# Attention beside a token-mixing MLP on one core: where a unit's dense matmuls stand

## The chip, the cores and the metric

The kernel runs on one core of a Trainium2 chip. The metric is the device time of one execution in microseconds. Three runs of the kernel before gave 650.64, 650.80 and 651.08; the median, 650.8, is the time before.

The core has five engines with a queue of instructions each: TensorE (PE in the profile, PEld for its weight loads), VectorE (DVE), ScalarE (ACT), GpSimd (POOL) and SyncE (SP), which here issues nearly all DMAs. The engines tell each other with semaphores when something is done.

## The reference

The input x has 2048 tokens of 1024 columns. Its layernorm `xn` goes through two blocks, and the sum is returned. Cut to what matters:

```python
xn = _layernorm(x)
# A: 32 heads of 32 columns, 4 segments of 512 tokens
q, k, v = xn @ wq, xn @ wk, xn @ wv
for s in range(4):
    p = softmax(q_s @ k_s.T * scale + causal_mask)
    a_dot = p @ v_s
    a_mem = (phi(q_s) @ M) / (phi(q_s) @ z + 1e-6)     # phi(t) = t + 1 if t > 0 else exp(t)
    o_s = g * a_mem + (1 - g) * a_dot                  # g = sigmoid(beta), per head
    M, z = M + phi(k_s).T @ v_s, z + sum(phi(k_s))
A = concat(o_s) @ wo
# B: an MLP across tokens, 2048 -> 3584 -> 2048, for each column
B = (gelu(layernorm(xn).T @ w1 + b1) @ w2 + b2).T
return x + A + B
```

## The kernel before, in words

The program has two large parts in time. Until about 387 us it computes the MLP (and the keys of the last two segments). From there on it runs attention, and only attention is touched by the change.

**Units.** Attention goes through 32 units (`N_UNIT`), u = 8 s + g: segment s of four, group g of four heads out of eight. In `attention` (the loop over `u`) each unit has:

- its logits, `logits(u, step)`: keys times queries into banks 0 to 3 of PSUM. Step 0 and step 1 belong to the unit, step 2 is done once for an even unit and its successor together. After the matmuls ScalarE takes the exp of all four banks into `pT` (line 1370, 128x2048), GpSimd masks the diagonal blocks (line 1374), and `late_exps` (line 1219, tile `etmp`) takes the exp that phi needs for every Q or K product that has ended since the last logits.
- the weighing of the unit before, `weigh(u - 1, 0..2)`: `pT` times the values, and phi(q) times the memory, into banks 4 and 5, which VectorE evacuates (lines 1424 and 1427, tile `ost`).
- the normalising of the unit before, `combine(u - 1)`, on VectorE: reciprocals, a product (line 1473, `prod`), an add (line 1479, `o_s`). Then a DMA transposes `o_s` into `oT`.
- dense jobs, eight matmuls of 128x512 each, which fill TensorE while ScalarE works on the exps.

**Dense jobs.** `unit_jobs(u)` says which jobs a unit adds to the queue `self.jobs`: a V product of the next segment (`v_job`), the Q product of unit u + 2 (`q_job`), its K product in the first two segments (`k_job`; later keys are loaded by `k_load`), and products of finished segments with wo (`wo_job`). From unit 18 (`QUOTA_FROM`) wo products are appended until the unit has 24 matmuls if even and 20 if odd; what the last of them has over the quota (`self.left`) is carried into the next unit. The last unit takes all that remains.

Jobs run in the order of the queue, in pieces: `dense(n)` takes the next n matmuls, whatever jobs they belong to. The loop calls it between the other pieces of the unit, and the sizes n come from `cut(total, shares)`, which divides the unit's matmuls by fixed shares. The seven shares of an even unit are for the places before logits 0, before `weigh` 0, 1 and 2, before logits 1, before logits 2, and after it; an odd unit has no logits 2 and six shares.

**Banks and evacuations.** A dense job takes bank 6 or 7 in turn when its first matmul is issued. When its eighth matmul is issued the job's `end` is emitted: the evacuation of its bank. V and (from the third segment on) all Q products are evacuated by ScalarE (lines 1299 and 1253), wo products by VectorE, which adds the product to a tile `fin` (line 1313) that already holds the residual and the MLP. A job's first matmul waits, by the bank's bookkeeping in `FW._waits`, for the evacuation of the job two before it. The end of a Q product also asks for the next weights of `wq` (`ring.ensure(u + 2)`), and puts the exp for phi on the list of `late_exps`.

**Side work.** Pieces of VectorE work of the unit (`combine`, phi of the queries in `phi_q`, scaling of later tokens) wait in `self.side`. After logits 1, `dense` pops one of them each time a job has reached one of its stops (`STOPS_FEW` in these units: after matmuls 1, 3, 5 and 7 of a job that ScalarE evacuates, after 1, 3 and 5 of one that VectorE evacuates). So the order of the jobs also sets the order of instructions on VectorE, ScalarE and the DMA queue. All queues are written out in this order when the program is built.

After unit 31 `tail` does the weighing of that unit and the wo products of the last segment.

Of the kernel before, what the change touches and what calls it, by code (L numbers as in the profile page):

```python
# [30 lines left out]
N_UNIT = N_SEG * N_GRP  # L31
# [355 lines left out]
class _Kernel:  # L387
# [1119 lines left out]
    def unit_jobs(self, u):  # L1507
        jobs = [self.wo_job(*self.wo_jobs.popleft())] if 10 <= u < self.QUOTA_FROM else []
        m = u // 4 + 1
        if m < 2 * N_SEG:  # L1510
            jobs.insert(0, self.v_job(m, u % 4))
        if u + 2 < N_UNIT:
            jobs.append(self.q_job(u + 2))
            if u + 2 < N_UNIT // 2:
                jobs.append(self.k_job(u + 2))
            else:
                self.k_load(u + 2)
        if u >= self.QUOTA_FROM:
            quota = self.QUOTA[u % 2] if u + 1 < N_UNIT else 100
            quota -= 8 * len(jobs) + sum(8 - j[0] for j in self.jobs)  # L1520
            while quota > 0 and self.wo_jobs:
                jobs.append(self.wo_job(*self.wo_jobs.popleft()))
                quota -= 8
            self.left = max(-quota, 0)
        return jobs
# [5 lines left out]
    def attention(self):  # L1531
        self.jobs, self.turn, self.left = deque(), 0, 0
        self.side, self.stops = deque(), self.STOPS
        self.exps, self.in_etmp = [], [None] * 4
        self.wo_jobs = deque((c, half) for c in range(4 * (N_SEG - 1)) for half in range(2))
        self.jobs.extend([self.q_job(0), self.k_job(0)] + [self.v_job(0, c) for c in range(4)])
        self.dense(16)
        self.late_exps()
        self.phi_k(0)
        self.k_transpose(0)  # L1540
        self.jobs.extend([self.q_job(1), self.k_job(1)])
        self.dense(100)
        for u in range(N_UNIT):
            if u == N_GRP:
                t, R = _Walk(self.mem, self.B_AT + self.STG_AT, self.B_AT + self.S2_AT).take(
                    "oT2", [P, N_GRP, SEG_L], BF16, N_GRP)
                self.oT.append(t)
                self.R_oT.append(R)
                self.load_fin(0)
                self.load_fin(1)  # L1550
            if 1 <= u <= N_GRP:
                self.fw.dma(self.wo[:, u - 1, :], self.A_wo[(u - 1) * P:u * P, :], writes=[self.R_wo[u - 1]])
            even = u % 2 == 0
            self.jobs.extend(self.unit_jobs(u))
            total = 8 * len(self.jobs) - sum(j[0] for j in self.jobs) - self.left
            xn = self.XN_AT.index(u) + 4 if u in self.XN_AT else None
            if u in self.XN_AT[::4]:
                self.xn_load(xn)
                self.xn_load(xn + 1)
            if u >= 18 and even:  # L1560
                cuts = self.cut(total, (0, 5, 1, 4, 0, 9, 5))
            elif u >= 18:
                cuts = self.cut(total, (4, 1, 2, 1, 0, 12))
            elif u < 10 or u >= 14 and total <= 26:
                cuts = self.cut(total, (0, 4, 2, 4, 1, 13, 8) if even else (7, 3, 2, 4, 1, 15))
            else:
                cuts = self.cut(total, (0, 4, 2, 2, 2, 14, 8) if even else (7, 3, 2, 2, 2, 16))
            end = u >= N_UNIT - 4
            self.stops = self.STOPS_FEW if total <= 26 and u >= 14 else self.STOPS
            self.dense(cuts[0])  # L1570
            self.logits(u, 0)
            self.dense(cuts[1], end)
            while end and self.side:
                self.side.popleft()()
            if u:
                self.weigh(u - 1, 0)
            self.dense(cuts[2], False)
            if u:
                self.weigh(u - 1, 1)
            self.dense(cuts[3], False)  # L1580
            if u:
                self.weigh(u - 1, 2)
                steps = self.combine(u - 1)
                last = steps[-1]
                steps[-1] = lambda u=u, last=last: (last(), self.o_transpose_dma(u - 1))
                self.side.append(steps.pop(0))
            if N_GRP <= u:
                self.side.append(lambda u=u: self.phi_q(u))
            if u:
                self.side.extend(steps)  # L1590
            if u + 1 < N_UNIT:
                self.side.append(lambda u=u: (self.phi_k(u + 1), self.k_transpose(u + 1)))
            if xn is not None:
                self.side.append(lambda c=xn: (self.xn_scale(c), self.xn_transpose(c), c % 4 < 2 and self.xn_load(c + 2)))
            self.dense(cuts[4])
            self.logits(u, 1)
            if even:
                self.dense(cuts[5])
                self.logits(u, 2)
            self.dense(8 * len(self.jobs) - sum(j[0] for j in self.jobs) - self.left)  # L1600
        while self.side:
            self.side.popleft()()
        self.tail()
# [84 lines left out]
```

## Time and profile before

| | |
|---|---|
| median of three runs | 650.8 us |
| the profiled execution | 650.74 us |
| its span, first to last instruction | 649.0 us |
| TensorE busy | 644.7 us, 99% |
| VectorE busy | 435.4 us, 67% |
| ScalarE busy | 282.8 us, 44% |
| GpSimd busy | 153.9 us, 24% |
| exp of the logits, line 1370, 80 instructions | 150.1 us, 1.877 each |
| granted TensorE clock | 1.00 |

How to read it: a line of the timeline has the start and the length in us, the engine, the line of the kernel, the operation, what is written and read, and how many instructions are merged in the line. Successive matmuls overlap, so a merged line of eight ends later than eight times their pitch. The span is shorter than the execution's time by 1.7 us, which lie around it. A line such as `[0.15 <-ACT pT L1370]` at the end tells how long the engine was idle before and which instruction ended that.

In the stretch from 500 to 550 us, which has units of the third segment, TensorE is busy for 50.0 us, VectorE for 43.7, ScalarE for 40.7 and GpSimd for 23.2.

### The profile page before, as it was taken

How to read it: one execution, taken by the hardware profiler on the slowest of the kernel's cores; microseconds unless marked ns; L12 is line 12 of the kernel's file. 1: busy time of each engine (PE TensorE's matmuls, PEld its weight loads, DVE VectorE, ACT ScalarE, POOL GpSimd, SP SyncE). 2: the span in 40 equal slices, each digit the busy share in tenths (PEclk: the TensorE clock that was granted, in tenths of full speed). 3: DMA queues.
4: the chain of work that ended last, by engine and by line, in shares of the span. 5: the costliest groups of instructions: out<-in, count | busy, mean ns of one | idle time of the engine just before them, and what ended most of it. 6: DMA issues, size and time to landing. Idle time of an engine off the chain costs nothing.

```text
span 649.0 us, 11186 instructions
## 1 busy us (share of the span) xinstructions
PE 644.7 (99%) x4611; PEld 304.2 (47%) x4611; DVE 435.4 (67%) x813; ACT 282.8 (44%) x307; POOL 153.9 (24%) x179
## 2 busy tenths in 40 slices
PE   9999999999999999999999999999999999999998
PEld 3444444444444444444444444444455455545544
DVE  6975676665556664744647325766887888887886
ACT  6543232232210000110101037778777878889860
POOL 2500000000001220220202203344334444554450
PEclk9999999999999999999999999999999999999999
DMA  9804233233489947538272947999854675445334
GB/s 303 217 0 131 66 100 96 65 108 87 125 249 205 239 123 211 143 116 227 68 224 84 270 120 179 177 175 225 140 136 102 160 166 122 126 105 130 100 97 139
DMA packets 190123, 95.00 MB, mean 146 GB/s; under 512 B 108664, under 2 KB 176248, under 8 KB 190072
## 3 DMA queue, kind: packets, MB, share of 16 engines
q1 hardware_dynamic: 189928, 94.25, 57.6%
q8 instruction: 36, 0.59, 0.4%
q14 instruction: 15, 0.12, 0.1%
q10 hardware_dynamic: 144, 0.03, 0.0%
HBM read 69.23 MB, written 11.53 MB: 124 GB/s over the span
## 4 chain that ended last, share of the span: by engine, by line
PE 96%; ACT 2%; DVE 1%; DMA 0%; POOL 0%; issue 0%; DVEq 0%
PE ps_all L199 96%; ACT pT L1370 2%; DVE ln_st L587 1%; DMA xin<-in_A_x_dram 0%; DVE h L627 0%; POOL ln_rs L611 0%; ACT qT L1253 0%; ACT vA L1299 0%; DVE ln_mv L590 0%; DVE ln_mv L609 0%; DVE fin L1634 0%; PE ps_all L205 0%; DVEq L70 0%
## 5 line engine op out<-in xcount | busy, mean ns | idle before, releaser
L1370 ACT ACTIVATE pT<-ps_all 128x2048 bf16<-128x2048 f32 x80 | 150.1, 1877 | 41.2 <-PE ps_all L199 41.0
L1374 POOL TENSOR_SCALAR_AFFINE_SELECT pT<-pT 128x512 bf16<-128x512 bf16 x128 | 105.3, 841 | 159.2 <-ACT pT L1370 159.2
L689 DVE TENSOR_TENSOR part<-ps_all,part 128x512 f32<-128x512 f32 x84 | 57.7, 690 | 108.5 <-PE ps_all L199 87.5
L1075 POOL TENSOR_TENSOR part<-part,stg 128x512 f32<-128x512 f32 x24 | 33.0, 1402 | 284.8 <-DVE part L689 284.8
L746 ACT ACTIVATE g<-part,b1c 128x512 f16<-128x512 f32 x36 | 26.0, 722 | 98.7 <-DVE part L689 98.7
L199 PE MATMUL ps_all<-wv,xnT 128*128 128x512 bf16 x256 | 68.7, 380 | 0.3 <-ACT qT L1253 0.2
L199 PE MATMUL ps_all<-xnT,wq 128*128 128x512 bf16 x256 | 65.3, 380 | 0.0
L199 PE MATMUL ps_all<-wo,oT 128*128 128x512 bf16 (+2 forms) x272 | 63.6, 367 | 0.0
L694 ACT ACTIVATE part<-ps_all 128x512 f32<-128x512 f32 x24 | 14.0, 597 | 101.8 <-PE ps_all L199 67.1
L199 PEld LDWEIGHTS ps_all<-vA,pT 128*128 128x128 bf16 x1280 | 46.0, 96 | 17.2 <-DVE ost L1424 0.4
L1424 DVE TENSOR_TENSOR ost<-ps_all,eps 128x396 bf16<-128x396 f32 (+1 forms) x72 | 37.0, 522 | 24.6 <-PE ps_all L199 23.6
L199 PE MATMUL ps_all<-g,w2s 128*128 128x512 f16 x224 | 51.0, 379 | 0.0
L199 PE MATMUL ps_all<-g,sum 128*128 128x512 f16 x224 | 51.0, 379 | 0.0
L199 PE MATMUL ps_all<-gT,sum 128*128 128x512 f16 x224 | 50.3, 379 | 0.0
L199 PE MATMUL ps_all<-vA,pT 128*128 128x33 bf16 x1280 | 48.4, 177 | 0.0
L199 PE MATMUL ps_all<-h,sum 128*128 128x512 f16 x192 | 45.2, 379 | 0.0
L199 PE MATMUL ps_all<-h,w1s 128*128 128x512 f16 x192 | 44.9, 379 | 0.0
L199 PE MATMUL ps_all<-hT,sum 128*128 128x512 f16 x192 | 43.6, 379 | 0.0
L1473 DVE TENSOR_TENSOR prod<-ost,srec 128x1024 bf16<-128x1024 bf16 (+1 forms) x31 | 36.2, 1166 | 0.3
L199 PEld LDWEIGHTS ps_all<-wo,oT 128*128 128x128 bf16 x272 | 23.9, 98 | 24.6 <-issue 3.9
L199 PEld LDWEIGHTS ps_all<-xnT,wq 128*128 128x128 bf16 x256 | 22.7, 97 | 26.9 <-issue 5.3
L199 PEld LDWEIGHTS ps_all<-g,w2s 128*128 128x128 bf16 x224 | 21.9, 98 | 26.4
(119 smaller groups left out, 863.9 us busy)
## 6 DMA issues: line engine op xcount, KB each, us to landing
w2s<-in_B_w_dram SPq DMA_DIRECT2D x8, 1792.0 KB, 9.8
w1s<-in_B_w_dram SPq DMA_DIRECT2D x12, 1024.0 KB, 5.6
wq<-in_A_wq_dram SPq DMA_DIRECT2D x32, 256.0 KB, 3.3
xs<-in_A_x_dram SPq DMA_DIRECT2D x24, 256.0 KB, 3.2
stg<-in_A_x_dram SPq DMA_DIRECT2D x16, 256.0 KB, 2.9
out_dram<-stg SPq DMA_DIRECT2D x16, 256.0 KB, 3.7
wk<-in_A_wk_dram SPq DMA_DIRECT2D x16, 256.0 KB, 3.5
fin<-out_dram SPq DMA_DIRECT2D x16, 256.0 KB, 3.1
```

Of the source, the lines that this page charges most:

```text
L199: ins = self.nc.tensor.matmul(*args, **kwargs)
L587: fw.op("dve", lambda e: e.bn_stats(st[:, 6 * h:6 * h + 6], src[:, 512 * h:512 * h + 512]), reads=[self.R_xin[c]], writes=[R])
L689: self.fw.op("dve", lambda e: e.tensor_tensor(self.tmp[dst][:], self.bank(b), self.tmp[src][:], op=ALU.add), reads=[self.R_bank[b], self.R ...
L694: self.fw.op("act", lambda e: e.activation(self.tmp[dst][:], self.bank(b), ACT.Copy), reads=[self.R_bank[b]], writes=[self.R_tmp[dst]])
L746: self.fw.op("act", lambda e: e.activation(self.gB[f % 2][half][:, f // 2, :], src, ACT.Gelu_apprx_tanh, bias=self.b1c[:, f:f + 1], scale= ...
L1075: fw.op("pool", lambda e: e.tensor_tensor(self.tmp[t][:], self.tmp[t][:], self.stg[k][:, 512 * half:512 * half + 512], op=ALU.add), reads= ...
L1370: fw.op("act", lambda e: e.activation(dst, src, ACT.Exp, scale=SCALE), reads=self.R_bank[0:4], writes=[R[v % 2][kb] for v, kb, _ in blocks ...
L1374: fw.op("pool", lambda e: e.affine_select(d, d, pattern=[[0, 4], [1, P]], compare_op=ALU.is_ge, fill=0.0, base=0, channel_multiplier=-1), ...
L1424: fw.op("dve", lambda e: e.tensor_tensor(dst, src, eps, op=ALU.add), reads=[self.R_bank[b], self.R_eps], writes=[self.R_ost[o][part]])
L1473: fw.op("dve", lambda e: e.tensor_tensor(self.prod[:, a0:a1], ost[:, a0:a1, 0:D_HEAD], rec[:, a0:a1].unsqueeze(2).to_broadcast([P, a1 - a0 ...
```

## The change

```diff
 def unit_jobs(self, u):
 ...
             while quota > 0 and self.wo_jobs:
-                jobs.append(self.wo_job(*self.wo_jobs.popleft()))
+                jobs.insert(-1 if u + 2 < N_UNIT else len(jobs), self.wo_job(*self.wo_jobs.popleft()))
                 quota -= 8
 ...
 def attention(self):
 ...
             if u >= 18 and even:
                 cuts = self.cut(total, (0, 5, 1, 4, 0, 9, 5))
-            elif u >= 18:
+            elif u >= 18 and u + 1 < N_UNIT:
                 cuts = self.cut(total, (4, 1, 2, 1, 0, 12))
+            elif u == 0:
+                cuts = self.cut(total, (0, 4, 2, 4, 0, 9, 5))
             elif u < 10 or u >= 14 and total <= 26:
                 cuts = self.cut(total, (0, 4, 2, 4, 1, 13, 8) if even else (7, 3, 2, 4, 1, 15))
```

It has three edits.

1. From unit 18 to unit 29 the wo products that a unit adds stand before its Q product, where they stood behind it. Units 30 and 31 have no Q product, and wo products are appended there as before. The order of the queue in units 19 to 21, with Q22 the Q product of unit 22 and O a wo product, was V Q21 O, V Q22 O, V Q23, and is V O Q21, V O Q22, V Q23. How many matmuls each place of a unit gets stays as it was.
2. Unit 0 gets shares of its own. Its 24 matmuls were cut into 0, 3, 1, 4, 0, 10, 6 and are cut into 0, 4, 2, 4, 0, 9, 5.
3. Unit 31 no longer takes the shares of the odd units from 18 on, and falls to the general branch. Its 16 matmuls were cut into 3, 1, 2, 0, 0, 10 and are cut into 4, 1, 1, 2, 0, 8.

## The prediction

> **What bounds the kernel.** I read the page's first part, then its chain of work, then that chain in order of time, then the timeline around the units where it leaves TensorE. The first two:
>
> ```profile
> PE 644.7 (99%) x4611; PEld 304.2 (47%) x4611; DVE 435.4 (67%) x813; ACT 282.8 (44%) x307; POOL 153.9 (24%) x179
> ...
> PE 96%; ACT 2%; DVE 1%; DMA 0%; POOL 0%; issue 0%; DVEq 0%
> ```
>
> TensorE sets the end, and the diff adds no matmul to it and takes none away. So the change is worth what it does to TensorE's waits. In attention (from 387 us) the chain leaves TensorE in few places:
>
> ```profile
> 387.89 1.89 ACT pT L1370
> ...
> 549.87 1.88 ACT pT L1370
> 551.75 0.49 ACT vA L1299
> 552.25 1.88 ACT pT L1370
> 554.13 0.50 ACT qT L1253
> 554.62 0.14 issue
> 554.76 24.56 PE ps_all L199 x314
> ...
> 624.37 1.89 ACT pT L1370
> ```
>
> Of these I need the idle time, not the length. In the timeline dense matmuls (128x512) follow one another every 0.216 us, and one that precedes logits takes 0.311 us to the logits' start. What exceeds these pitches is a wait. Between 387 and 634 us five exceed them by over 0.01 us: 0.22 us before unit 0's second logits (389.82), 0.25 us at 554.76 (unit 21's first V matmul, behind the Q copy), 0.16 us at 584.15 (the same in unit 25), 0.21 us before unit 31's first logits (626.30) and 0.06 us before its second (628.68). Together 0.90 us: no reordering of attention's matmuls can win more than that, 0.14%.
>
> Below, Q22 is the Q product of unit 22, V and O the products with wv and wo, L0, L1, L2 a unit's logits. Dense jobs alternate between banks 6 and 7, so a job's first matmul waits until the evacuation of the job two before it is done. Two stretches show how little room that leaves. From unit 19's L1 into unit 20:
>
> ```profile
> 542.33 0.40 PE L199 MATMUL ps_all<-qT,kT 32*128 32x384 bf16 x8
> ...
> 544.40 1.03 PE L199 MATMUL ps_all<-wo,oT 128*128 128x512 bf16 x4
> ...
> 544.73 1.72 DVE L1473 TENSOR_TENSOR prod<-ost,srec 128x512 bf16<-128x512 bf16 x2
> ...
> 546.49 0.74 DVE L1479 TENSOR_TENSOR o_s<-prod 128x512 bf16<-128x512 bf16 x1
> 546.55 0.38 PE L199 MATMUL ps_all<-wv,xnT 128*128 128x512 bf16 x1
> ...
> 547.15 0.68 DVE L1313 TENSOR_TENSOR fin<-ps_all,fin 128x512 bf16<-128x512 f32 x1
> ```
>
> VectorE works without a pause from 542.43, and the add that evacuates O (fin, L1313) comes at 547.15. That is after V has started at 546.55; today V doesn't need it, since its bank was Q21's. And from unit 20's L1 into unit 21:
>
> ```profile
> 549.42 0.40 PE L199 MATMUL ps_all<-qT,kT 32*128 32x384 bf16 x8
> ...
> 551.64 0.59 ACT L1299 ACTIVATE vA<-ps_all 128x512 bf16<-128x512 f32 x1
> ...
> 552.25 1.88 ACT L1370 ACTIVATE pT<-ps_all 128x2048 bf16<-128x2048 f32 x1
> 552.36 1.89 PE L199 MATMUL ps_all<-wo,oT 128*128 128x512 bf16 x8
> ...
> 554.18 0.39 PE L199 MATMUL ps_all<-qT,kT 32*128 32x512 bf16 x4
> ```
>
> The row at 552.36 starts 0.13 us after the V copy that frees its bank; 554.18 starts 0.05 us after the exp that frees banks 0 to 3. ScalarE has no room here: exp, V copy, exp, Q copy, back to back.
>
> **What the skill says.** The Trainium skill, PSUM — Partial Sum Buffer, section "Engine vs sequencer instructions", calls the ScalarE and VectorE queues strict FIFO and has matmuls start in program order. So one evacuation emitted behind a long instruction holds TensorE. The trace agrees: at 554.76 V waits for a Q copy that stood behind an exp of 1.88 us. Its section "PSUM bank collisions raise a hardware error" asks for a semaphore per bank, which is what ties job n+2 to job n. TensorE: Matmul & The Clock Gate, section "Wait — 56ns, not 53.3ns?", gives 215.7 ns from start to start for 512 columns; this trace has 215 to 216.
>
> **The change, part by part.** Instructions and their durations stay, and TensorE's order changes.
>
> *Unit 0.* Cuts go from 0,3,1,4,0,10,6 to 0,4,2,4,0,9,5. L0 at 387.44, then ten matmuls where eight were: 387.44 + 0.32 + 10 x 0.216 + 0.10 = 390.02 for L1, and exp ends at 389.77: no wait. Then nine and L2 at 392.40 (before 392.41), exp of L1 just done; then ten to unit 1's L0 where eleven were: 395.00 for 395.22. Gain **0.22**; POOL's selects and the copies keep over 0.3 us of room.
>
> *Unit 31.* The shares fall to the branch below: with 16 matmuls, 4,1,1,2,0,8 for 3,1,2,0,0,10. Between unit 30's L2 and L0 nine matmuls fill what eight left idle (L0 stays at 626.30). L1 has four behind L0 for three, comes at 628.84 and finds its exp done at 628.63. Both waits go: **0.27**. The tail then arrives 0.27 us sooner; its first weighing needs a POOL select finished near 632.4 and starts near 633.5.
>
> *Units 18 to 29, Q last.* O jobs take the place of Q in the first half. The two old waits at 554.76 and 584.15 go, since V's bank is then an O's: **0.41** gained. Q's loads of wq on SP's queue move behind the transposes of oT and pk, and kT's loads change places with them; they landed 3 to 4 us after issue (556.39 to 560.24), and Q24 starts some 10 us after. No price, and the cover is that distance. New waits:
>
> (a) Odd into even units (19/20, 23/24, 27/28): the job before Q is now O, so V20, V24 and O in unit 28 wait for fin. O's end is popped behind both prod instructions, ahead of o_s. fin can start where prod ends (544.73 + 1.72 = 546.45; consecutive VectorE rows overlap by up to 0.08), so 546.4, ends at 547.1, and with 0.05 to 0.14 us from an evacuation's end to its matmul TensorE starts at 547.16 where it was ready at 546.55: **0.61**. Unit 23: 574.21 + 1.72 gives 576.64 against 576.03: **0.61**. Unit 27 has no memory update on VectorE: 602.51 + 1.72 gives 604.95 against 604.74: **0.21**. Each may be off by 0.1 to 0.15. Queued behind the waiting matmul is all of TensorE.
>
> (b) Even into odd units (20/21, 24/25): Q21 and Q25 end after unit 20's and 24's L0, no longer before. Their exp for phi (etmp, L1219, 0.62 us a row) is emitted behind the next logits, which now is L1: exp of L1, etmp, V copy, exp of L2. A copy's row of 0.59 costs ScalarE 0.50 (551.75 to 552.25), the rest overlapping its neighbour, so etmp costs about 0.51. V's copy ends at 552.74 for 552.23, Q22, which takes that bank, starts 0.5 late, and L0 at 554.69 also meets an exp of L2 that is 0.51 late: one delay, not two. **0.51** twice. In unit 28 etmp takes the place of Q30's copy: nothing.
>
> (c) O in unit 29 waits for a fin behind prod and another fin, which my addition ends between 612.3 and 612.6, against TensorE at 612.47: 0 to 0.3, take **0.05**. The Q copy now stands before the exp of L0 in units 21, 25 and 29 and delays it by 0.15 (560.21 to 560.81 shows that order, 0.60 for the usual 0.45). It ends 2.47 after L0, and L1 comes at 2.54 or more: nothing, barely.
>
> Sum: -0.22 - 0.27 - 0.41 + 1.43 + 1.02 + 0.05 = **+1.6 us**. The profiled execution took 650.74 (span 649.0, 1.7 around it) and the runs' median is 650.8, so I forecast **652.4** (+0.25%).
>
> **Rivals.** *Gains alone:* if fin and etmp find room that I don't see (VectorE's chain beginning sooner after L1, or TensorE delayed elsewhere), the 0.90 us stand: 649.9, not slower. It is decided by where fin ends: before 546.4 there is no wait. Against it: the chain of eight VectorE rows from 542.43 is tied to L1 and has no gap. *Only one of the two waits:* (b) alone gives +0.17 with (c), 650.9; (a) alone +0.58, 651.3. For it speaks that both rest on tenths of a microsecond. *Waits that feed others:* a later exp of L1 in odd units, a kT or oT transpose that lands late (the last oT landed at 638.24, used from 638.9, and the tail now comes 0.27 sooner), a few more of 0.3: 653.6. *No effect at all* would need TensorE to run ahead of every wait; the pitches exclude it.
>
> **Numbers.** Both waits as priced 0.64, one only 0.18, gains alone 0.08, further waits 0.10. About 0.2% (1.3 us) is what a measurement of this kernel can tell from no change. The likeliest case has its own range, 651.9 to 652.9, of which some four fifths lie above 652.1. Slower by more than 0.2%: 0.64; within: 0.34; faster: 0.02, as 0.90 us isn't 1.3. The range for eight in ten, 651.0 to 653.3, takes in one wait only and half of the further waits.
>
> **What would show it.** In the changed profile: L1 of unit 0 without a wait and unit 31's first logits without one; waits of about 0.6 us of V20 and V24 for fin L1313, 0.2 in unit 28; about 0.5 us of Q22 and Q26 for the V copy L1299, with an etmp between the exp and that copy. I am wrong if fin runs before prod there, if etmp stands behind L2, or if waits appear before unit 18.

## The result and the profile after

| | before | after |
|---|---|---|
| median | 650.93 us | 652.83 us |
| lowest and highest | 650.64 to 651.08 | 652.51 to 652.93 |
| profiled execution | 650.74 us | 652.73 us |
| its span | 649.0 us | 651.0 us |

The ratio of the times is 1.0029, with a 95% interval of 1.0016 to 1.0042. The kernel became 1.9 us slower, 0.29%, where about 0.2% can be told from no change; the interval's lower end is a little below that. There are six runs of each, and those of the kernel before take in the three from which 650.8 was the median. The forecast was 652.4.

First the profile page of the kernel after: the busy times of the engines, and the shares of the chain of work that ended last.

```profile
PE 639.0 (98%) x4559; PEld 303.4 (47%) x4611; DVE 435.1 (67%) x813; ACT 282.0 (43%) x307; POOL 152.7 (23%) x179
...
PE 93%; DVE 3%; issue 2%; ACT 1%; DMA 0%; POOL 0%; DVEq 0%
```

Two things must be read with care here. TensorE's busy time is lower than before by 5.7 us, and yet the kernel is slower: 4559 matmuls are recorded beside 4611 weight loads, so 52 records are missing. Where one is missing, its neighbours stand two pitches apart, which leaves 0.05 or 0.16 us that look idle. These holes make up about half of the "issue" share (time for which the profile shows nothing that the engine waited for), 11.0 us in all. Another 4.05 us of it are four stretches of 0.79 to 1.40 us just ahead of a `fin`, in which VectorE runs `prod`. So what is real is the part of VectorE in the chain: 3% and these four stretches, where it was 1%. The same chain in order of time shows where it enters:

```profile
546.32 0.69 DVE fin L1313
...
576.74 0.69 DVE fin L1313
...
606.07 0.69 DVE fin L1313
...
614.03 0.69 DVE fin L1313
```

Three times, 30 us apart, the chain goes from the normalising on VectorE into `fin`: these are the ends of units 19, 23 and 27. The last row belongs to unit 28, and another `fin` stands before it at 610.43, with a normalising between the two: the place of the prediction's term (c). The timeline of the kernel after at the first of them, which answers to the rows from 542.33 on that the prediction shows:

```profile
544.68 1.72 DVE L1473 TENSOR_TENSOR prod<-ost,srec 128x512 bf16<-128x512 bf16 x2
...
545.63 1.04 PE L199 MATMUL ps_all<-xnT,wq 128*128 128x512 bf16 x4
546.32 0.68 DVE L1313 TENSOR_TENSOR fin<-ps_all,fin 128x512 bf16<-128x512 f32 x1
546.92 0.41 DVE L1479 TENSOR_TENSOR o_s<-prod 128x512 bf16<-128x512 bf16 x1
547.15 0.38 PE L199 MATMUL ps_all<-wv,xnT 128*128 128x512 bf16 x1 [0.48 <-DVE fin L1313]
```

Four matmuls of Q21 from 545.63 at 0.216 bring TensorE to 546.50. V20 starts at 547.15, so it waits 0.65 us, for `fin`, which ends at 547.00. And the timeline from unit 20's L1 into unit 21, which answers to the rows from 549.42 on (L1 is now at 550.01):

```profile
552.23 0.62 ACT L1219 ACTIVATE etmp<-qT 128x512 bf16<-128x512 bf16 x1
...
552.72 0.39 PE L199 MATMUL ps_all<-wo,oT 128*128 128x512 bf16 x1
552.75 0.59 ACT L1299 ACTIVATE vA<-ps_all 128x512 bf16<-128x512 f32 x1
...
553.70 1.67 PE L199 MATMUL ps_all<-xnT,wq 128*128 128x512 bf16 x7 [0.59 <-ACT vA L1299]
```

`etmp` stands between the exp and the V copy, as the prediction said, and Q22 waits for that copy. (The row at 553.70 has seven matmuls, since the record of the first is missing; its weights were loaded at 553.46. From O's last matmul, 552.72, two pitches lead to 553.15, and the second matmul of Q22 is at 553.70, so the wait is 0.55 us.)

The old idle places are gone in the shares that were changed. TensorE's timeline of the kernel after, the second logits of unit 0 and the first of unit 31:

```profile
390.19 0.40 PE L199 MATMUL ps_all<-qT,kT 32*128 32x384 bf16 x8
...
628.60 0.40 PE L199 MATMUL ps_all<-qT,kT 32*128 32x512 bf16 x4
```

Neither has a wait beside it. The row at 628.60 follows the last of nine wo matmuls (the first of them at 626.55; one has no record) by the 0.311 us that precede logits.

Set side by side by the starts of the exps, from unit to unit, and for unit 31 by the start of the transposes in `tail`, the two traces differ in eight places. The beginning of attention, which the change does not touch, came 0.15 us later; that offset was between -0.13 and +0.31 us in the experiments, and differences "by the trace" below are taken without it.

| place | after minus before |
|---|---|
| unit 0 | -0.21 us |
| V20 waits for fin | +0.65 |
| units 20 to 21: Q22's wait less the old wait at 554.76 | +0.29 |
| V24 waits for fin | +0.57 |
| units 24 to 25: Q26's wait less the old wait at 584.15 | +0.37 |
| O in unit 28 waits for fin | +0.25 |
| O in unit 29 waits for the second fin | +0.22 |
| unit 31 | -0.28 |
| sum | +1.86 |

With the offset this is +2.01 us, and the spans, taken to 0.01 us, differ by 2.02: nothing of size lies elsewhere.

### The profile page after: what moved, and what is told of

Same layout as the page of the kernel before. It is cut to its first block, busy times and chain, and to the rows that moved or that the text cites. A ratio compares the mean times of both kernels' runs of the same rounds, so it can differ in the third digit from the quotient of the medians.

```text
span 651.0 us, 11126 instructions
## 1 busy us (share of the span) xinstructions
PE 639.0 (98%) x4559; PEld 303.4 (47%) x4611; DVE 435.1 (67%) x813; ACT 282.0 (43%) x307; POOL 152.7 (23%) x179
## 4 chain that ended last, share of the span: by engine, by line
PE 93%; DVE 3%; issue 2%; ACT 1%; DMA 0%; POOL 0%; DVEq 0%
PE ps_all L199 93%; ACT pT L1370 1%; DVE fin L1313 1%; DVE ln_st L587 1%; DMA xin<-in_A_x_dram 0%; DVE pqT L1230 0%; DVE h L627 0%; DVE prod L1473 0%; POOL ln_rs L611 0%; DVE ost L1424 0%; DVE srec L1467 0%; ACT etmp L1219 0%; ACT vA L1299 0%; DVE mtmp L1228 0%; DVE srec L1468 0%
## 5 line engine op out<-in xcount | busy, mean ns | idle before, releaser
L199 PE MATMUL ps_all<-wv,xnT 128*128 128x512 bf16 x239 | 65.2, 380 | 2.0 <-DVE fin L1313 0.9
L199 PE MATMUL ps_all<-wo,oT 128*128 128x512 bf16 (+2 forms) x257 | 61.8, 366 | 1.7 <-issue 0.8
L199 PE MATMUL ps_all<-xnT,wq 128*128 128x512 bf16 x242 | 61.2, 380 | 1.9 <-ACT vA L1299 1.2
L199 PEld LDWEIGHTS ps_all<-gT,sum 128*128 128x128 f16 x224 | 21.8, 98 | 26.7 <-DVE gT L663 0.5
```

The source lines that it names most:

```text
L199: ins = self.nc.tensor.matmul(*args, **kwargs)
```

## The experiments

The theory is the prediction's: two new waits, (a) of V for a late `fin` and (b) of Q22 for a V copy behind a late `etmp`, each with a cost of its own, with the gain of the shares beside them. The rivals: the shares cost rather than gain; each moved Q product costs alike; the two waits cover for each other, so that taking one away gives nothing; VectorE or ScalarE have no room for any other order.

| kernel | edit | median (before, same chip) | ratio, 95% interval | by the trace |
|---|---|---|---|---|
| e1_q_last | edit 1 alone | 653.26 (650.68) | 1.0038, 1.0026 to 1.0051 | +2.33 us |
| e2_shares | edits 2 and 3 alone | 650.20 (650.68) | 0.9992, 0.9984 to 1.0001 | -0.50 |
| e6_even_last | after, edit 1 in even units up to 26 alone | 649.87 (650.68) | 0.9987, 0.9981 to 0.9994 | -0.85 |
| e7_odd_last | before, edit 1 in odd units alone | 653.34 (650.68) | 1.0041, 1.0029 to 1.0054 | +2.66 |
| e0_after | after | 652.47 (650.76) | 1.0027, 1.0016 to 1.0038 | +1.85 |
| e3_fin_first | after, fin ahead of prod | 651.12 (650.76) | 1.0007, 0.9999 to 1.0015 | +0.37 |
| e4_etmp_later | after, in units 20 and 24 etmp left for the next unit's L0 | 651.58 (650.76) | 1.0012, 1.0005 to 1.0018 | +0.81 |
| e5_both | both | 650.15 (650.76) | 0.9990, 0.9982 to 0.9998 | -0.67 |
| e10_no_29 | e5, units 28 and 29 no longer end in Q | 650.35 (650.80) | 0.9994, 0.9986 to 1.0002 | -0.42 |
| e11_etmp_28 | e10, the same in unit 28 too | 649.95 (650.78) | 0.9987, 0.9981 to 0.9994 | -0.85 |

The intervals of e2_shares, e3_fin_first and e10_no_29 take in 1, and those of kernels that lie a few tenths of a microsecond apart partly overlap. Such differences rest on the traces, one of each kernel. How well a trace repeats is seen in e0_after: every step of the table above comes again within 0.01 us.

### The edits apart

The order of the queue alone (e1_q_last), and the shares alone (e2_shares):

```diff
-                jobs.append(self.wo_job(*self.wo_jobs.popleft()))
+                jobs.insert(-1 if u + 2 < N_UNIT else len(jobs), self.wo_job(*self.wo_jobs.popleft()))
```

> Only the first edit: Q last in units 18 to 29, the shares of units 0 and 31 as before. My theory: the new waits of the changed kernel's trace stay (0.65 + 0.57 + 0.25 for the fin adds, 0.29 and 0.37 net for the late phi exp, 0.22 in unit 29), the 0.49 us from the shares is missing: 2.3 us over the kernel before, 653.3. Rival, the new shares of the last unit cost the time: no slower than before, 650.5 to 650.9.

```diff
-            elif u >= 18:
+            elif u >= 18 and u + 1 < N_UNIT:
                 cuts = self.cut(total, (4, 1, 2, 1, 0, 12))
+            elif u == 0:
+                cuts = self.cut(total, (0, 4, 2, 4, 0, 9, 5))
```

> Only the shares of units 0 and 31, Q where it was. My theory: 0.21 us won in unit 0 and 0.28 in unit 31, 0.49 in all, 650.4. Rival, the shares cost time: 651.5 or more. In the trace the exps of units 1 to 30 should all stand 0.21 us sooner relative to unit 0's first exp.

Measured: +2.58 us in the median and +2.33 by the trace for the order, -0.48 and -0.50 for the shares. In e1_q_last the six places of units 19 to 29 are as in the kernel after (0.65, 0.29, 0.57, 0.37, 0.25, 0.22 us), and in e2_shares only units 0 and 31 differ from before (-0.21 and -0.28). By the traces the shares don't cost time, and the two parts add up: 2.33 - 0.50 = 1.83 for 1.86.

### Even and odd units apart

Each moved Q product either costs alike, or it is the place that decides. e6_even_last is the kernel after with the Q product last in even units up to 26 only; e7_odd_last is the kernel before with it last in odd units only:

```diff
-                jobs.insert(-1 if u + 2 < N_UNIT else len(jobs), self.wo_job(*self.wo_jobs.popleft()))
+                jobs.insert(-1 if u % 2 == 0 and u < 28 else len(jobs), self.wo_job(*self.wo_jobs.popleft()))
```

> The changed kernel with Q last only in the even units 18 to 26. My theory puts both new waits into the odd units' order, and the 0.41 us of removed waits into the even units': so all gains without the losses, 0.90 us under the kernel before, 650.0, at most 0.1 lost to unit 21's V behind a fin. Rival, each Q that is moved behind an O costs alike: half of 2.35 less the shares' 0.49, 651.6.

```diff
-                jobs.append(self.wo_job(*self.wo_jobs.popleft()))
+                jobs.insert(-1 if u % 2 and u + 2 < N_UNIT else len(jobs), self.wo_job(*self.wo_jobs.popleft()))
```

> Q last only in the odd units 19 to 29, shares as before. My theory: fin waits of 0.65, 0.57 and 0.25 us in units 20, 24 and 28, late phi exps of 0.5 us in units 20 and 24, none of the gains: 2.5 us over the kernel before, 653.4. Rival, each moved Q costs alike: 652.1.

They end on opposite sides of the kernel before. With the Q product last in these even units, what remains of the waits of TensorE from 387 to 620 us is this (the columns: total us, how many, the longest):

```profile
PE ps_all L199 <- issue: 2.7, 17, 0.2
```

These are the holes of missing records, 0.16 us each on the mean (the view lists idle times from 0.15 us on). The kernel after, from 387 to 640 us, has the same row, and besides those of V20, V24 and O in unit 29 for `fin`, and of Q22 and Q26 for the V copy:

```profile
PE ps_all L199 <- DVE fin L1313: 1.2, 4, 0.5
PE ps_all L199 <- ACT vA L1299: 1.2, 2, 0.6
```

(One of the four `fin` rows, 0.16 us in unit 31, is again the hole of a missing record. The wait of O in unit 28 leaves less than 0.15 us idle, since the row before it reaches into it.) So nearly the whole loss comes from the odd units; only the 0.22 in unit 29 follows from unit 28, which e6_even_last leaves as it was: e7_odd_last, where unit 28 has the old order too, doesn't have that step. When an odd unit ends in Q, the job before the next V is an O, whose `fin` is late (a), and that Q product ends after the next L0, so that its `etmp` falls behind L1 (b). When an even unit ends in Q, the V of the next unit is freed by a `fin` instead of by a Q copy, and the old waits at 554.76 and 584.15 go: 0.85 - 0.50 = 0.35 us is the gain beside the shares. e6_even_last is faster than both kernels, by 0.8 us than before.

e7_odd_last cost 2.66 us, 0.2 more than expected. Its steps in units 20 and 24 are 0.64 + 0.39 and 0.57 + 0.39 us; unit 28 has 0.24 + 0.46, where the kernel after has 0.25. The 0.46 was not counted: where unit 28 doesn't end in its Q product, Q30's copy still stands behind the exp of L1, and the late `etmp` of Q29 delays it.

The two halves don't simply add up. Once the odd units are changed, the step from unit 20 into 21 is +0.39 us with Q22 at its old place (e7_odd_last) and +0.29 with Q22 last (the kernel after), and that from 24 into 25 is +0.39 and +0.37. So beside the odd units' new order that of the even ones is worth 0.10 and 0.02 us at these places, where it won 0.20 and 0.15 alone.

### Each wait taken away

The kernel after was run again beside these. For (a), `prod` is popped later in three units, so that O's `fin` goes ahead of it; for (b), the exp for phi is left in two units for the first logits of the next unit. The third kernel has both.

> The changed kernel itself once more, beside the three that follow, as their measure: 1.9 us over the kernel before, 652.8.

```diff
             self.stops = self.STOPS_FEW if total <= 26 and u >= 14 else self.STOPS
+            if u in (19, 23, 27):
+                self.stops = ((1, 3, 5, 7), (1, 3))
```

> The changed kernel, but in units 19, 23 and 27 a job that VectorE evacuates pops side work only after its matmuls 1 and 3, so that the fin add comes ahead of the two prod instructions. My theory: the waits for fin in units 20, 24 and 28 go (0.65 + 0.57 + 0.25 = 1.47 us), the waits of Q22 and Q26 stay: 0.45 us over the kernel before, 651.4. Rival, VectorE has no room in these units at all: the wait moves to the ost adds and the time stays at 652.8.

```diff
 def logits(self, u, step):
 ...
-        self.late_exps()
+        if u not in (20, 24) or step == 0:
+            self.late_exps()
```

> The changed kernel, but in units 20 and 24 the exps for phi aren't taken behind the second and third logits and so fall behind the first logits of the next unit. My theory: Q22 and Q26 start without a wait (0.54 us each), nothing else moves but a little ScalarE delay in units 21 and 25: 1.0 to 1.1 us under the changed kernel, 651.8. Rival, the V copies or the exps of the third logits are late for another reason: 652.8.

> Both of the last two in the changed kernel. My theory: all new waits but the 0.22 us of unit 29 go and the gains stay: 2.55 us under the changed kernel, 650.3, 0.6 under the kernel before. Rival, one wait takes the place of the other since both lie on one chain: about 651.4.

The timeline of e3_fin_first at the end of unit 19:

```profile
544.58 0.68 DVE L1313 TENSOR_TENSOR fin<-ps_all,fin 128x512 bf16<-128x512 f32 x1
545.18 1.88 DVE L1473 TENSOR_TENSOR prod<-ost,srec 128x512 bf16<-128x512 bf16 x2
...
545.53 1.04 PE L199 MATMUL ps_all<-xnT,wq 128*128 128x512 bf16 x4
546.40 0.38 PE L199 MATMUL ps_all<-wv,xnT 128*128 128x512 bf16 x1
```

`fin` has moved from 546.32 to 544.58, and V starts 0.87 us after the first of the last four matmuls of Q21, four pitches, with no wait. The normalising, now behind it, costs TensorE nothing. Against the kernel after this is -1.49 us by the trace, for the 1.47 that the three waits measured. The timeline of e4_etmp_later in unit 20:

```profile
552.12 0.59 ACT L1299 ACTIVATE vA<-ps_all 128x512 bf16<-128x512 f32 x1
...
552.73 1.88 ACT L1370 ACTIVATE pT<-ps_all 128x2048 bf16<-128x2048 f32 x1
553.07 1.67 PE L199 MATMUL ps_all<-xnT,wq 128*128 128x512 bf16 x7
...
557.03 1.15 ACT L1219 ACTIVATE etmp<-qT 128x512 bf16<-128x512 bf16 x2
```

The V copy follows its exp directly, and Q22 is at its pitches again. The two `etmp` come together at 557.03, and nothing waits for them. Against the kernel after: -1.05 us, for the 0.55 that each of the two waits measured.

Both together give -2.53 us, against -1.49 - 1.05 = -2.54. The waits are independent, none takes the other's place, and both engines have room for the work in another order. What e5_both still has is the step into unit 29.

### The step into unit 29

It was to go if units 28 and 29 no longer end in their Q product:

```diff
-                jobs.insert(-1 if u + 2 < N_UNIT else len(jobs), self.wo_job(*self.wo_jobs.popleft()))
+                jobs.insert(-1 if u < 28 else len(jobs), self.wo_job(*self.wo_jobs.popleft()))
```

> The kernel with both new waits removed, and units 28 and 29 have Q ahead of O again, so that no O of unit 29 waits for the second fin of unit 28. My theory of the 0.22 us lost there: it goes and nothing takes its place, 0.2 us under the kernel that keeps it, 649.9 to 650.0, 0.8 under the kernel before, with no step between the exps of units 28 and 29. Rival, the step comes from the Q copy ahead of the first exp of unit 29: that copy is gone too, but the V-less units lose elsewhere: 650.2. The exps can't tell these two causes apart by their sum alone; the fin row and the first O of unit 29 in the trace can.

This missed. The step into unit 29 is gone, 0.00 for 0.22 us, yet the kernel lost 0.25 us against e5_both, because a new wait of 0.46 us stands in unit 28. The timeline of e10_no_29:

```profile
609.32 0.62 ACT L1219 ACTIVATE etmp<-qT 128x512 bf16<-128x512 bf16 x1
...
609.81 0.39 PE L199 MATMUL ps_all<-wo,oT 128*128 128x512 bf16 x1
609.84 0.59 ACT L1253 ACTIVATE qT<-ps_all 128x512 bf16<-128x512 f32 x1
...
610.49 1.90 PE L199 MATMUL ps_all<-wo,oT 128*128 128x512 bf16 x8 [0.29 <-ACT qT L1253]
```

Unit 27 still ends in Q29, whose `etmp` comes behind L1 of unit 28, and with Q30 at its old place its copy is behind that `etmp`. It is mechanism (b) in a third unit, and the same 0.46 as in e7_odd_last. If that is so, leaving `etmp` for later there must give it back:

```diff
-        if u not in (20, 24) or step == 0:
+        if u not in (20, 24, 28) or step == 0:
```

> As the run before, and unit 28 too takes no exp for phi behind its second and third logits. My theory: the 0.46 us wait there is the late exp for phi of Q29 once more, since Q29 is still the last job of unit 27; it goes, and the first O of unit 29 has no wait for fin either: 649.9, 0.9 under the kernel before, no step between the exps of units 28 and 30. Rival, Q30's copy alone is late at that place: 650.35 as before.

It did, -0.43 us to -0.85 by the trace. The timeline of e11_etmp_28 at the same place, where the Q copy starts at 609.09 and nine O matmuls run without a gap:

```profile
609.58 2.12 PE L199 MATMUL ps_all<-wo,oT 128*128 128x512 bf16 x9
```

e11_etmp_28 and e6_even_last reach the same gain, -0.85 us, by opposite ways: one keeps the new order in the odd units and moves what it makes late, the other does not make it late.

## Why the prediction was right, and where it was off

**The bound.** That no reordering of attention's matmuls can win more than 0.90 us was not contradicted: the two best kernels won 0.85 by the trace, and 0.8 in the median.

**Units 0 and 31.** Forecast -0.22 and -0.27, measured -0.21 and -0.28; e2_shares has them alone.

**The waits that go.** Forecast -0.41. With the new order in even units up to 26 only, the gain beside the shares was 0.35. Some 0.06 is left, of which 0.03 is a wait of V21.

**(a) Odd into even units.** Forecast 0.61, 0.61 and 0.21, measured 0.65, 0.57 and 0.25: each within 0.04, their sum 1.47 for 1.43. e3_fin_first took 1.49 away with nothing but `fin` moved ahead of `prod`, which shows the cause.

**(b) Even into odd units.** Forecast 0.51 twice, measured 0.55 twice before the old waits are taken off. The prediction priced `etmp` at 0.51 from the part of a neighbouring row that does not overlap. Its row is 0.62 and it moved the V copy's start by 0.52 (552.23 to 552.75). The Trainium skill, ScalarE: Activation LUTs, section "What ACT_TABLE_LOAD costs", has back-to-back ACTIVATEs overlap by about 93 ns, which this agrees with. That L0 of the odd unit meets an exp that is just as late, one delay and not two, was right as well: e4_etmp_later gave back 1.05 us for the two.

**Unit 28 at nothing** held because Q29 and Q30 were both moved. e7_odd_last and e10_no_29 moved Q29 without Q30 and paid 0.46. The cover that the prediction named, `etmp` in the place of Q30's copy, was the right one.

**(c) O in unit 29** is the term that was mis-sized: 0.05 taken, from bounds of 0 to 0.3, and 0.22 measured. The prediction gives the bounds and not the addition behind them; what it says of the whole change, that instructions and their durations stay, does not hold here. The product of this place in the timeline of the kernel before, and its select:

```profile
609.38 1.22 DVE L1473 TENSOR_TENSOR prod<-ost,srec 128x1024 bf16<-128x1024 bf16 x1
...
609.77 2.09 POOL L1374 TENSOR_SCALAR_AFFINE_SELECT pT<-pT 128x512 bf16<-128x512 bf16 x2 [3.21 <-ACT pT L1370]
```

And in that of the kernel after:

```profile
611.85 4.11 POOL L1374 TENSOR_SCALAR_AFFINE_SELECT pT<-pT 128x512 bf16<-128x512 bf16 x4 [3.46 <-ACT pT L1370]
...
612.45 1.66 DVE L1473 TENSOR_TENSOR prod<-ost,srec 128x1024 bf16<-128x1024 bf16 x1
614.03 0.68 DVE L1313 TENSOR_TENSOR fin<-ps_all,fin 128x512 bf16<-128x512 f32 x1
...
614.77 0.39 PE L199 MATMUL ps_all<-wo,oT 128*128 128x512 bf16 x1 [0.15 <-DVE fin L1313]
```

`prod` took 1.66 here. With 1.22, `fin` would have ended 0.44 us sooner, at 614.27, and O, for which TensorE was ready at 614.54 (0.32 after the L0 at 614.22), would not have waited. `prod` also stands later: the first `fin` (at 610.43) is now ahead of the normalising, so `prod` begins 2.99 us after L1 of unit 28 (609.46), where it began 2.00 after it (607.38), and a select has begun before it. That this made it longer is argued in the last section, not shown.

**The sum.** +1.86 by the trace, +1.90 in the medians, for +1.6 forecast. Of the 0.26 by which the trace exceeds it, 0.17 is (c), 0.08 is (b) and 0.04 is (a); these are 0.03 too much, which the rounded readings leave open. The rival with gains alone fell because `fin` ended at 547.00, behind 546.4 (without the offset and the gain of unit 0 it is 547.06, where the prediction has 547.1); the rival with one wait only, because both were there and independent; further waits did not come beyond (c). wq's loads and kT's, which changed places on SP's queue, cost nothing that the traces show: the view of the waits has none of TensorE for a DMA from 387 to 640 us.

## What to carry to other kernels

Where jobs alternate between two banks, moving one job changes what the job two after it waits for, so write down for each neighbour whose evacuation frees its bank, and behind what that evacuation is queued. An order that is good in one kind of unit can cost in the other: ask for each kind apart, since here the even units up to 26 won 0.35 us alone and the odd ones lost 2.5 to 2.7. A late evacuation can be mended on the evacuating engine's queue (fin ahead of prod, etmp behind the copy) rather than by giving up the order of the matmuls; but look again after each repair, as e10_no_29 uncovered one more case of the same wait.

## What the runs showed of the hardware

`prod` over 128x1024 (line 1473) took one of two times at the place of (c), the normalising of unit 27 in unit 28: 1.65 or 1.66 us in the kernel after, its repetition, e1_q_last, e3_fin_first, e4_etmp_later and e5_both, and 1.22 us in before, e2_shares, e6_even_last, e7_odd_last, e10_no_29 and e11_etmp_28. A GpSimd select (line 1374) runs beside it in all of them. In the first group it starts 0.6 us ahead of `prod` (611.85 and 612.45 in the kernel after), in the second 0.39 us behind it (609.77 and 609.38 before). The kernel before alone shows the same division: of its 17 products of this size, the eight ahead of which a select had begun, and still ran, took 1.51 to 1.66 us. The nine others took 1.22, whether a select began with them or later (505.66, 609.38) or none ran beside them (470.51).

The add `o_s` (line 1479) at the end of unit 19 took 0.74 us in before, where a select runs from 545.87 to 546.95 beside it, and 0.41 us in the kernel after and 0.42 in e3_fin_first, where none does. That select took 1.08 us, and selects with no VectorE instruction beside them took 0.63 to 0.64. The Trainium skill, SBUF — State Buffer, section "Who interferes with whom", says that a VectorE instruction with two inputs in SBUF contends with a GpSimd instruction that reads SBUF. Both `prod` and `o_s` have two such inputs and the select reads one, so these times speak for it; no run here moved the selects alone, and so the cause stays argued.

In the kernel after, from the end of an evacuation to the start of the matmul that waited for it passed 0.06 us behind three `fin` (ends and starts 577.42 and 577.48, 606.75 and 606.81, 614.71 and 614.77) and 0.15 us behind the first (547.00 and 547.15), and 0.14 us behind ScalarE (the V copy ended at 553.34; Q22's first matmul is put at 553.48, one pitch before the second). In the kernel before it was 0.14 behind one Q copy (554.62 and 554.76) and 0.05 or 0.06 behind the other (584.09 and 584.15). What decides between the two is open.
